# A state-space mixer with an MLP gate: one small product in two column halves, two broadcasts by DMA, and another order of the work

## The chip, the cores and the metric

One core of a Trainium2 chip runs the whole kernel. The time is the device time of one execution in microseconds. The kernel before was timed three times: 156.28 us in the median, from 156.19 to 156.82.

## What is computed

One sequence of 2048 rows with 448 features. The rows are normalized; a linear state-space scan and an MLP with GELU both read the normalized rows, and the MLP's SiLU gates the scan's output:

```python
xn  = layernorm(x)
dt  = exp(log_dt);  Lam_bar = exp(dt * Lambda)            # complex, 448 states
B_bar = ((Lam_bar - 1) / Lambda)[:, None] * B
Bu  = einsum("bld,pd->blp", xn, B_bar)
h_t = Lam_bar * h_{t-1} + Bu_t                            # over 2048 rows
s   = 2 * einsum("blp,dp->bld", h, C).real + xn * Dskip
y   = gelu(layernorm(xn) @ w1 + b1) @ w2 + b2             # 448 -> 1792 -> 448
out = x + s * silu(y)
```

All inputs and the output are bfloat16.

## The kernel before, in words

The rows go in four groups g of 512: two blocks b of 128 partitions, and in each partition two neighbouring rows, "par" 0 and 1. The scan runs over pairs of rows: an output row of par 1 needs the state after its pair (matrix CQ, seven 128-row pieces), a row of par 0 the state before it (CZ) and its own input through the direct matrix M0 (448 x 448, with D/2 on its diagonal).

The stages and their lines:
- Opening: loads, statistics (L402, L403), normalization (L423), transposes on TensorE (L426), short matmuls that only keep TensorE busy (L393), columns of b1 by matmul (L570, L571).
- First MLP product, `mm1_run` (L756). The contraction of 448 is split into row halves of the array, 64 rows each. Each pair of hidden blocks has a phase A of six matmuls and a phase B of eight, then two GELUs on ScalarE (L760) that free the two PSUM banks.
- Second MLP product, `mm2` (L778): fourteen matmuls of 448 columns. VectorE adds b2 (L781); for groups 0 and 3 ScalarE takes SiLU (L783), for 1 and 2 a tanh (L785) and a VectorE product (L786). ScalarE's function tables are switched between them (L414, L590, L594).
- `rows` (L576): two matmuls with one row each (L580) spread b2 and D over the partitions, into PSUM banks 6 and 5; copies (L581, L582) write b2bc and dbc (with the factor 0.5).
- Parameters of the scan (L496 on): small operations on 128x4 tiles on POOL or VectorE. A sine polynomial gives lr and li, from which come the combinations of B (`lb`, L635 and L637, then DMA transposes into BT) and of C (`cq`, L634 to L637: CQ0 to CQ6, CZ0 to CZ6).
- `m0` (L670): four pieces of the direct matrix, each seven matmuls of 448 columns (L673) and one short one for the diagonal (L675), copied by L390. The last piece, d = 3, has 64 rows.
- `bu` (L684): the scan's input, with BT0 to BT6, fourteen matmuls of 256 columns for each pair of pieces; copies u0 to u3 (L390).
- `ssm` (L696): products with the turning table WT, the scans (L708, L710) and products back into h, nearly all on VectorE; POOL or VectorE carry the end of a group over (L719 to L722).
- `ym` (L808): the output, L821 and L824 for par 0, L821 and L827 for par 1; then L833, L835 or L838 and the addition of x (L841) on VectorE or POOL, and the store.

The order of the work is written out by hand. The program makes a list of tasks, each with its reads and writes. `link` derives what each waits for. `ORDER` gives the order in which the tasks are issued, as numbers in that list, so every engine's queue is fixed; `SECOND` lists the tasks that take their second choice of engine. In `emit`, a task waits for one value of each semaphore that it needs and its engine has not waited for already. Every engine has one semaphore, every DMA one of its own. SP issues nearly all DMAs, among them the transposes; POOL issues the two loads of b1.

Of the kernel before, what the change touches and what calls it, by code (L numbers as in the profile page):

```python
# [7 lines left out]
ACT = mybir.ActivationFunctionType  # L8
# [27 lines left out]
class Plan:  # L36
# [69 lines left out]
    def emit(self):  # L106
# [5 lines left out]
        done = {}  # L112
        settle = [t for t in order if t.eng == "sp"][-5]
        for t in order:
# [25 lines left out]
            done[t] = (t.sem, self.counts[t.sem])  # L140
# [29 lines left out]
""".split()]  # L170
SECOND = [int(k) for k in """
29 52 54 58 61 63 70 71 72 75 76 79 80 83 84 86 87 88 89 106 130 133 135 161 163 164 188 192 193 196 228 230 232 244 248 252 253 263 273 336 348 353
361 371 373 375 385 398 399 400 433 441 443 446 447 465 479 480 484 488 492 496 498 501 505 507 522 527 528 586 602 628
# [4 lines left out]
X0 L1 N1 S1 W0 S0 R1 W1 Z0 B00 B01 M0 M1 B02 M2 B03 M3 X1 L2 B10 B11 B12 B13 R2 Y000 Y001 Y010 Y011 N2 W2 Z1 X2 L3 Y100 Y101 Y110 Y111 N3 Z2 X3 B20 B21 B22 B23 R3 S3 W3 B30 B31 B32 B33 Y200 Y201 Y210 Y211 Z3 Y300 Y301 Y310 Y311  # L178
# [12 lines left out]
def bass_recurrent_scan__ssm_conv_s5__mixer_channel_mlp__prompt_kernel(  # L191
# [17 lines left out]
    kb = Plan(nc)  # L209
    with ExitStack() as es:  # L210
# [84 lines left out]
        with nc.Block():  # L295
# [48 lines left out]
            for par in range(2):  # L344
                ld("sp", x_all[:, 0, par, :], dram_ap(A_x, par * D, [[2 * D, 128], [1, D]]), [f"x0p{par}"], 114688, S1)
# [12 lines left out]
            for k, vec in enumerate((B_b2, A_Dskip)):  # L358
                ld("sp", vrows[64 + 32 * k:65 + 32 * k, 64:512], dram_ap(vec, 0, [[D, 1], [1, D]]), [f"vr{3 + k}"], 1000, 0)
# [29 lines left out]
            def copy(pairs, rd, wr):  # L389
                kb.either(("act", [lambda e, o=o, i=i: e.activation(o, i, ACT.Copy) for o, i in pairs]), ("dve", [lambda e, o=o, i=i: e.tensor_copy(o, i) for o, i in pairs]), rd, wr)  # L390
# [576 lines left out]
```

## Time and profile before

The profiled execution took 156.18 us; its span is 154.4 us and 1.78 us lie around it. The granted clock is 1.0 throughout. From the page and the answers of the trace:

| what | value |
|---|---|
| timed runs | 156.28 us (156.19 to 156.82) |
| profiled execution / span | 156.18 / 154.4 us |
| ScalarE, POOL busy | 94.9 us (61%), 34.6 us (22%) |
| L756, 462 matmuls | 45.2 us |
| L778, 224 matmuls | 44.4 us |
| L684, 196 matmuls | 24.0 us |
| L821, 110 matmuls | 22.4 us |
| first L756 / end of the last matmul of the chain | 6.95 / 149.99 us |

"Busy" counts the time in which an instruction of an engine runs; matmuls are pipelined and their ends are modelled, so the distance from one to the next is often shorter than the stated length. The same holds on VectorE, where an operation of 0.68 us is often followed after 0.60. The chain of waits goes back from the last instruction to what released each step; a step that is on it sets the end.

### The profile page before, as it was taken

The page shows a single profiled execution, that of the slowest core. Times are in us where ns is not written, and L with a number is a line of the kernel's source. Part 1 is how long each engine was busy: PE and PEld are TensorE (multiplying, and loading weights), DVE is VectorE, ACT ScalarE, POOL GpSimd, SP SyncE. Part 2 cuts the span into 40 slices and gives each one's busy share as a digit, 9 for nine tenths or more (in the row PEclk, how much of TensorE's full clock was granted, in tenths as well). Part 3 has the DMA queues.
Part 4 walks back from the last instruction along what each step waited for, and adds up shares of the span by engine and source line. Part 5 has one row for each costly group of instructions (what it writes and reads, how often), then busy time and mean ns, then how long its engine had stood idle before and what let it go on. Part 6 is the DMA issues. An engine that isn't in the chain of part 4 may idle for free.

```text
span 154.4 us, 3113 instructions
## 1 busy us (share of the span) xinstructions
PE 149.3 (97%) x1140; PEld 89.0 (58%) x1140; DVE 134.9 (87%) x290; ACT 94.9 (61%) x178; POOL 34.6 (22%) x81
## 2 busy tenths in 40 slices
PE   7999999999999999999999999989999999999991
PEld 6777855455566576645444556755455565655561
DVE  3859899499898999999989998998989376999974
ACT  3797998988977757918927870115378661473200
POOL 6125850121300000000013950720030070002012
PEclk9999999999999999999999999999999999999999
DMA  4999669889893062200011310380031001000122
GB/s 121 290 310 373 182 140 261 148 156 219 183 172 69 4 125 84 46 4 2 0 39 25 59 59 7 62 185 4 0 59 59 6 0 62 0 0 4 59 111 69
DMA packets 31146, 14.52 MB, mean 94 GB/s; under 512 B 24722, under 2 KB 30746, under 8 KB 31130
## 3 DMA queue, kind: packets, MB, share of 16 engines
q1 hardware_dynamic: 30916, 14.26, 39.3%
q8 instruction: 9, 0.15, 0.4%
q10 hardware_dynamic: 150, 0.05, 0.1%
q14 instruction: 7, 0.06, 0.1%
q0 software_dynamic: 64, 0.00, 0.0%
HBM read 6.66 MB, written 1.84 MB: 55 GB/s over the span
## 4 chain that ended last, share of the span: by engine, by line
PE 92%; DVE 4%; issue 1%; ACT 1%; POOLq 0%; DVEq 0%
PE psum L756 28%; PE psum L778 28%; PE psum L684 12%; PE psum L821 12%; PE psum L824 4%; PE psum L673 4%; PE psum L393 3%; DVE g_sb L786 1%; PE psum L426 1%; PE psum L827 1%; DVE vs L722 1%; DVE xn_sb L467 1%; DVE t L835 1%; ACT gT L760 1%; DVE t L838 0%
## 5 line engine op out<-in xcount | busy, mean ns | idle before, releaser
L756 PE MATMUL psum<-xn2T,w_sb 64*128 64x512 bf16 (+1 forms) x462 | 45.2, 345 | 0.3
L778 PE MATMUL psum<-w_sb,gT 128*128 128x448 bf16 x224 | 44.4, 353 | 0.0
L760 ACT ACTIVATE gT<-psum,b1f 128x512 bf16<-128x512 f32 (+1 forms) x66 | 36.1, 625 | 10.1 <-PE psum L756 10.0
L756 PEld LDWEIGHTS psum<-xn2T,w_sb 64*128 64x128 bf16 x462 | 25.4, 109 | 18.7 <-issue 3.4
L778 PEld LDWEIGHTS psum<-w_sb,gT 128*128 128x128 bf16 x224 | 21.8, 98 | 20.1 <-issue 0.6
L684 PE MATMUL psum<-xnT,BT 128*128 128x256 bf16 x196 | 24.0, 273 | 0.1
L390 ACT ACTIVATE u_sb<-psum 128x512 bf16<-128x512 f32 (+2 forms) x20 | 9.9, 496 | 20.0 <-PE psum L684 20.0
L684 PEld LDWEIGHTS psum<-xnT,BT 128*128 128x128 bf16 x196 | 18.6, 98 | 5.7 <-issue 1.5
L841 POOL TENSOR_TENSOR tmp<-t,x_all 128x448 bf16<-128x448 bf16 x7 | 8.8, 1274 | 31.6 <-DVE t L838 25.5
L708 DVE TENSOR_TENSOR_SCAN s_w<-dk,vs 128x774 f32<-128x774 f32 x8 | 14.1, 1759 | 0.0
L821 PE MATMUL psum<-CZ,h_sb 128*128 128x448 bf16 x56 | 11.9, 353 | 0.5 <-DVE Cr L833 0.5
L390 ACT ACTIVATE vs<-s_w 64x256 bf16<-64x256 f32 (+2 forms) x14 | 7.8, 567 | 6.5 <-DVE s_w L710 5.6
L781 DVE TENSOR_TENSOR o<-psum,b2bc 128x448 f32<-128x448 f32 x16 | 9.8, 619 | 2.1 <-PE psum L778 2.0
L719 POOL TENSOR_TENSOR ang<-s_w,ang 128x16 f32<-128x16 f32 x3 | 1.0, 330 | 45.4 <-ACT s_w L717 45.4
L468 ACT ACTIVATE xn_sb<-x_all,lnw 128x448 bf16<-128x448 bf16 (+2 forms) x16 | 9.8, 651 | 2.0 <-DVE lnw L453 0.7
L821 PE MATMUL psum<-CQ,h_sb 128*128 128x448 bf16 (+2 forms) x54 | 10.5, 332 | 0.0
L786 DVE SCALAR_TENSOR_TENSOR g_sb<-th,o 128x448 bf16<-128x448 f32 x8 | 6.6, 823 | 4.3 <-ACT th L785 4.3
L467 DVE TENSOR_SCALAR xn_sb<-x_all,lnw 128x448 bf16<-128x448 bf16 (+2 forms) x24 | 8.7, 393 | 0.1
L783 ACT ACTIVATE g_sb<-o 128x448 bf16<-128x448 f32 x8 | 4.5, 571 | 6.8 <-DVE o L781 6.7
L821 PEld LDWEIGHTS psum<-CZ,h_sb 128*128 128x128 bf16 x56 | 5.3, 98 | 5.4 <-DVE Cr L833 0.8
L634 ACT ACTIVATE tmp<-Cr,cw 128x448 f32<-128x448 bf16 (+1 forms) x11 | 7.2, 665 | 1.7 <-DVE CQ L637 1.3
L821 PEld LDWEIGHTS psum<-CQ,h_sb 128*128 128x128 bf16 x54 | 5.1, 98 | 4.0 <-DVE vs L703 0.4
(159 smaller groups left out, 197.3 us busy)
## 6 DMA issues: line engine op xcount, KB each, us to landing
out_dram<-tmp SPq DMA_DIRECT2D x7, 224.0 KB, 1.9
x_all<-in_A_x_dram SPq DMA_DIRECT2D x3, 448.0 KB, 4.1
w_sb<-in_B_w_dram SPq DMA_DIRECT2D x3, 448.0 KB, 7.0
w_sb<-in_B_w_dram SPq DMA_DIRECT2D x3, 384.0 KB, 5.0
vs<-in_A_C_re_dram SPq DMA_DIRECT2D x1, 392.0 KB, 4.4
Bn<-in_A_B_re_dram SPq DMA_DIRECT2D x1, 336.0 KB, 7.9
Bn<-in_A_B_im_dram SPq DMA_DIRECT2D x1, 336.0 KB, 8.2
vs<-in_A_C_im_dram SPq DMA_DIRECT2D x1, 336.0 KB, 4.1
```

The costliest lines, as they stand in the source:

```text
L390: kb.either(("act", [lambda e, o=o, i=i: e.activation(o, i, ACT.Copy) for o, i in pairs]), ("dve", [lambda e, o=o, i=i: e.tensor_copy(o, i ...
L467: on = [("dve", [lambda e, o=o, i=i: e.tensor_scalar(o, i, rs, nb, op0=ALU.mult, op1=ALU.add) for o, i in parts], 0.4, 0.12), ("act", [lam ...
L468: ("act", [lambda e, o=o, i=i: e.activation(o, i, ACT.Identity, bias=nb, scale=rs) for o, i in parts], 0.75, 0.2)]
L684: fns = [lambda e, r=r, m=m, d=d: e.matmul(psum[:, 4, r * NK:(r + 1) * NK], BT[:, m, d, :], xnT[:, gx, d, :], start=(d == 0), stop=(d == 6 ...
L708: dve(lambda e, so=so, vi=vi: e.tensor_tensor_scan(so, dk[:].rearrange("p i c -> p (i c)"), vi, 0.0, ALU.mult, ALU.add), ["v", "vl", "dk", ...
L756: return lambda e: e.matmul(view(bk[k]), w1_sb[rows, d, fcol(2 * j + k)], rhs[rows, d, :, :], start=not second and n == 0, stop=second and ...
L760: act([lambda e, k=k: e.activation(gT[:, gb, 2 * j + k, :].rearrange("p (r c) -> p r c", r=2)[:, :, cols], view(bk[k]), ACT.Gelu_apprx_tan ...
L778: fns = [lambda e, fi=fi: e.matmul(psum[:, bk, 0:D], gT[:, gb, fi, q * 128:(q + 1) * 128], w2_sb[:, fi, :], start=(fi == 0), stop=(fi == N ...
L781: dve(lambda e: e.tensor_tensor(o2[:, fb, :], psum[:, bk, 0:D], b2bc[:], ALU.add), [f"ps{bk}", "b2bc"], [f"oo{fb}"], 0.62, prio - 76)
L786: dve(lambda e: e.scalar_tensor_tensor(out=g_sb[:, gs, :], in0=th[:, fb, :], scalar=1.0, in1=o2[:, fb, :], op0=ALU.add, op1=ALU.mult), [f" ...
L821: fns = [lambda e, k=k: e.matmul(psum[:, bk, c0:c1], h_sb[:, hb, k, k0:k0 + 128], cm[:, k, c0:c1], start=(k == 0), stop=False) for k in ra ...
L841: add = lambda e: e.tensor_tensor(o_sb[:, ob, par * D + c0:par * D + c1], t3[:, fb, c0:c1], res, ALU.add)
```

## The change

Five things:
- `m0` for d = 3 becomes `m0_halves`: the seven matmuls go alternately to output partitions 0 to 63 and 64 to 127 of one bank, the diagonal one to the second half. The second half is copied to a tile in SBUF, and VectorE adds the two into M0.
- b2 and D are spread over the partitions by two DMA loads from POOL's queue, and D is halved in place; `rows` is not called any more, and SP's two small loads go.
- `emit`: a task's needs are sorted by the place of their producers in the order (DMAs count as 24 places later). What the producer's engine had itself waited for counts as known, so some waits are left out; those that stay are issued with the latest last.
- The step list keeps its content: the switches of ScalarE's tables are named in another way and fall on the same groups (SiLU for 0 and 3). The switch for group 3 no longer waits for the tiles th.
- New `ORDER` and `SECOND`.

```diff
@@ emit
-            need = {}
-            for d in t.deps:
+            waits = []
+            for d in sorted(t.deps, key=at.get, reverse=True):
                 sem, val = done[d]
-                if need.get(sem, 0) < val:
-                    need[sem] = val
-            for sem, val in need.items():
                 if seen.get(sem, 0) < val:
-                    eng.wait_ge(self.sems[sem], val)
-                    seen[sem] = val
+                    waits.append((sem, val))
+                    for s, v in knows[d].items():
+                        learn(seen, s, v)
+                    learn(seen, sem, val)
+            for sem, val in reversed(waits):
+                eng.wait_ge(self.sems[sem], val)
+            base = dict(seen)
...
-            done[t] = (t.sem, self.counts[t.sem])
+            done[t], knows[t] = (t.sem, self.counts[t.sem]), base
@@ loads
-            for k, vec in enumerate((B_b2, A_Dskip)):
-                ld("sp", vrows[64 + 32 * k:65 + 32 * k, 64:512], dram_ap(vec, 0, [[D, 1], [1, D]]), [f"vr{3 + k}"], 1000, 0)
+            ld("pool", b2bc[:], dram_ap(B_b2, 0, [[0, 128], [1, D]]), ["b2bc"], 114688, -50, reads=["sgn3", "w1r_3"])
+            ld("pool", dbc[:], dram_ap(A_Dskip, 0, [[0, 128], [1, D]]), ["dbc"], 114688, -20, reads=["b2bc"])
+            kb.either(("act", lambda e: e.activation(dbc[:], dbc[:], ACT.Copy, scale=0.5), 0.6, 0.2),
+                      ("dve", lambda e: e.tensor_scalar(dbc[:], dbc[:], 0.5, None, op0=ALU.mult), 0.2, 0.12), ["dbc"], ["dbc"], -20)
@@ direct matrix
+            def m0_halves(bank):
+                BM = (3, 0, 4, 1, 5, 2, 6)
+                fns = [lambda e, k=k, m=m: e.matmul(psum[k % 2 * 64:k % 2 * 64 + 64, bank, 0:D], Bn[:, m, D + 384:896], CQ[:, k, :], start=(k < 2), stop=(k == 6))
+                       for k, m in enumerate(BM)]
+                fns.insert(6, lambda e: e.matmul(psum[64:128, bank, 384:D], ident[:, 0:64], De[:, 3, 0:64], start=False, stop=True))
+                pe(fns, [...], [f"ps{bank}"])
+                k = tslot[0] % 2
+                tslot[0] += 1
+                copy([(tmp[0:64, k, :], psum[64:128, bank, 0:D])], [f"ps{bank}"], [f"tmp{k}"])
+                dve(lambda e: e.tensor_tensor(M0[0:64, 3, :], psum[0:64, bank, 0:D], tmp[0:64, k, :], ALU.add), [f"ps{bank}", f"tmp{k}", "M0p"], ["M03"])
...
             def m0(d, bank, prio):
                 n = (128, 128, 128, 64)[d]
+                if d == 3 and 1:
+                    return m0_halves(bank)
@@ main program
             first_apply(1)
-            rows()
```

More of the change, by code (lines that the diff above doesn't have):

```diff
@@ L111, in emit, with learn @@
         assert len(order) == len(set(order)) == len(self.tasks)
-        done = {}
+        done, knows = {}, {}
+        at = {t: i + (24 if t.sem not in ENGS and not t.sem.startswith(("gelu", "silu")) else 0) for i, t in enumerate(order)}
         settle = [t for t in order if t.eng == "sp"][-5]
+        def learn(seen, sem, val):
+            if seen.get(sem, 0) < val:
+                seen[sem] = val
         for t in order:
@@ L344, in bass_recurrent_scan__ssm_conv_s5__mixer_channel_mlp__prompt_kernel @@
             for par in range(2):
-                ld("sp", x_all[:, 0, par, :], dram_ap(A_x, par * D, [[2 * D, 128], [1, D]]), [f"x0p{par}"], 114688, S1)
+                ld("sp" if par or not 0 else "act", x_all[:, 0, par, :], dram_ap(A_x, par * D, [[2 * D, 128], [1, D]]), [f"x0p{par}"], 114688, S1)
             ldx(1, 1, S1 + 2)
@@ L387, in tcols, with copy @@
                 return xn2_sb[:, b, a:a + 128]
-            def copy(pairs, rd, wr):
+            def copy(pairs, rd, wr, by=None):
+                if by is not None:
+                    kb.either(("act", [lambda e, o=o, i=i: e.activation(o, i, ACT.Copy, scale=by) for o, i in pairs]),
+                              ("dve", [lambda e, o=o, i=i: e.tensor_scalar(o, i, by, None, op0=ALU.mult) for o, i in pairs]), rd, wr)
+                    return
                 kb.either(("act", [lambda e, o=o, i=i: e.activation(o, i, ACT.Copy) for o, i in pairs]), ("dve", [lambda e, o=o, i=i: e.tensor_copy(o, i) for o, i in pairs]), rd, wr)
@@ L422, in first_apply @@
                     key = xk(0)[par:par + 1] if b == 0 else xk(1)
-                    dve(lambda e, src=src, dst=dst, mean=mean, r1=r1: e.tensor_scalar(dst, src, mean, r1, op0=ALU.subtract, op1=ALU.mult),
+                    parts = [(dst, src)] if b == 0 or not 0 else [(dst[:, 0:384], src[:, 0:384]), (xn2_sb[:, b, par * 512 + 384:par * 512 + 512], src[:, 320:D])]
+                    dve([lambda e, o=o, i=i, mean=mean, r1=r1: e.tensor_scalar(o, i, mean, r1, op0=ALU.subtract, op1=ALU.mult) for o, i in parts],
                         key + [f"r1{q}", f"mv0_{q}"], [f"xm{b}p{par}"])
+                    if b and 0:
+                        if par:
+                            kb.dma("sp", xn2T[:, 0, :, 128:256], xn2_sb[:, 1, :], reads=["xm1p0", "xm1p1", "xm1"], writes=["xmT1p0", "xmT1p1"], transpose=True)
+                        continue
                     bank, oap = 6 - par, xn2T[:, 0, par * 4:par * 4 + 4, b * 128:b * 128 + 128]
@@ L590, in silu_table, with gelu_again @@
                 kb.add("act", lambda e: e.preload_act_table_set("silu_and_others"), rd, [f"Ws{g}"], sem=f"silu{g}")
-            def gelu_again():
-                kb._sem("gelu")
-                kb.add("act", lambda e: e.preload_act_table_set("gelu_apprx_tanh_and_others"), ["W"] + [f"g{n}" for n in range(4)], ["Wg"], sem="gelu")
+            def gelu_again(g):
+                kb._sem(f"gelu{g + 1}")
+                kb.add("act", lambda e: e.preload_act_table_set("gelu_apprx_tanh_and_others"), ["W"] * (g == 0) + [f"g{n % 8}" for n in range(4 * g, 4 * g + 4)] * (9 >> g & 1), [f"Wg{g + 1}"], sem=f"gelu{g + 1}")
             def tables():
@@ L844, in part @@
                     on = [("dve", add, 0.1 + (0.28, 0.47)[par] * w / D, 0.12), ("pool", add, 0.2 + 1.1 * w / D, 0.15)]
-                    kb.either(*on, rd, [f"o{ob}_{par}_{c0}"], prio)
+                    if last and par or 1:
+                        kb.either(*on, rd, [f"o{ob}_{par}_{c0}"], prio)
+                    else:
+                        dve(add, rd, [f"o{ob}_{par}_{c0}"], on[0][2], prio)
                     if last:
@@ L871, in bass_recurrent_scan__ssm_conv_s5__mixer_channel_mlp__prompt_kernel @@
             first_apply(1)
-            rows()
-            mm1_run(0, None, range(N1, 7), [j % NP for j in range(N1, 7)])
+            if N1 < 7:
+                mm1_run(0, None, range(N1, 7), [j % NP for j in range(N1, 7)])
             mm1_run(0, 1, range(N1), [(j + 7) % NP for j in range(N1)])
@@ L922, in bass_recurrent_scan__ssm_conv_s5__mixer_channel_mlp__prompt_kernel @@
                 elif k == "S":
-                    if g == 0:
-                        gelu_again()
-                    if g == 3:
-                        silu_table(3, [f"gT1_{fi}_{b}" for fi in range(NF) for b in range(2)] + ["th0", "th1"])
+                    if a == "g" and wg(g + 1) == g + 1:
+                        gelu_again(g)
+                    if a == "s" and silu_now(g):
+                        silu_table(g, [f"gT{g % 2}_{fi}_{b}" for fi in range(NF) for b in range(2)])
                 elif k == "M":
```

17 lines of the change are left out of this document (10 added, 7 removed), and 34 rows, old and new, of the table ORDER.

## The prediction

> **What bounds the kernel.** I read four views. The page's first lines come first, because they tell which engine has no room left.
>
> ```profile
> span 154.4 us, 3113 instructions
> PE 149.3 (97%) x1140; PEld 89.0 (58%) x1140; DVE 134.9 (87%) x290; ACT 94.9 (61%) x178; POOL 34.6 (22%) x81
> PEclk9999999999999999999999999999999999999999
> ```
>
> TensorE is busy 97% at the full granted clock, so nothing can come from the clock. VectorE, at 87%, is the one that can stop it. Then I read the chain of work that ended last, in order of time (start, us, what).
>
> ```profile
> 17.34 0.29 PE psum L580 x2
> ...
> 61.44 1.44 PE psum L673 x7
> 62.88 0.03 PE psum L675
> ...
> 100.43 0.55 DVE Cr L833
> 100.98 0.05 issue
> 101.03 1.50 PE psum L821 x7
> ...
> 119.04 1.64 PE psum L684 x14
> ...
> 126.87 1.53 PE psum L684 x14
> ...
> 149.99 0.03 issue
> ```
>
> From 1.12 to 149.99 us the chain is nearly all TensorE, back to back; 4.4 us of VectorE, POOL and the last store follow. So an edit is worth what it takes from TensorE's stream, or puts into it as a wait. Third, the waits, to see how much of the stream is idle:
>
> ```profile
> PE psum L821 <- DVE Cr L833: 0.5, 1, 0.5
> ```
>
> This is the largest wait of a matmul after the start. The chain around it goes through VectorE from 96.2 to 101.0, and the fourth view, VectorE's timeline, shows why VectorE is late there:
>
> ```profile
> 96.91 2.02 POOL L841 TENSOR_TENSOR tmp<-t,x_all 128x448 bf16<-128x448 bf16 x2 [6.02 <-DVE vs L722]
> 96.95 1.03 DVE L722 TENSOR_TENSOR vs<-cur,vs 128x6 bf16<-128x6 f32 x1
> ```
>
> The same operation takes 0.18 at 80.89. While POOL works on 128x448 tiles here, three VectorE operations in a row (L722, L467, L786) each take about 0.8 longer than elsewhere.
>
> The sums go against the profiled execution: 156.18, that is the span of 154.4 and 1.78 around it. It lies 0.10 under the median of 156.28, and I add this 0.10 at the end.
>
> **The change, part by part.** I numbered the tasks by the program's text, before and after, and read both orders engine by engine.
>
> *Broadcasts.* The two L580 matmuls go: the chain gives 0.29, with the changes of form on both sides. ScalarE has its L581 copy (0.58) out of that stretch and another normalization (0.65) in, behind the two GELU pairs that free the banks TensorE still needs, so I take -0.29 (bounds -0.29 and 0). In place come two loads on POOL's queue and a scaling on ScalarE (0.58, as L581). The first load waits for a w1 load, the second for the first; both must be issued before POOL goes on to the sine polynomial. The trace has no load of 112 KB from POOL; the nearest rows are POOL's b1 loads (0.53 to 0.79 to issue, 2.9 and 3.8 to landing) and SP's 112 KB loads (2.1). The w1 load is issued at about 5.7 and lands, as the 64 KB rows do, 4.6 to 5.1 later; then come 0.8, 3 to 4 and 0.5 for the two loads, so the sine starts at 14.5 to 16 instead of 12.7. Late next would be the Bn combinations and through them the transposes; VectorE reaches its first need (lr) only near 20.5 in the new order, and the polynomial takes 3.1. That is the cover; if the load landed only after 7.0, like the 448 KB rows, 1 to 2 us would come onto VectorE there, of which the transposes (done 3 us ahead of the first L756 that reads them) and the table switch hide all but some 0.3. I take 0 (bounds 0 and +0.3).
>
> *The last 64 rows.* Now seven 448-column matmuls and a short one take 1.47 (61.44 to 62.91). In two column halves four go to one half and three and the short one to the other. No row shows column halves. From below: the row halves of L756 run in pairs, so that the chain has 84 of 512 columns in 9.38, 0.112 each, where L778 at full width has 14 of 448 columns in 2.65, 0.189 each, which would be 0.216 for 512. With that overlap it is 4 x 0.189 = 0.76, and 0.87 with the 0.11 of a change of form (next part). From above: no overlap, 1.47. I take 0.87, so -0.60 (bounds -0.71 and 0). The new copy and add (0.5 and 0.6 on VectorE) are counted below. The result is needed only at the first L824, ten us later.
>
> *Changes of form.* After row-split work (L756) fourteen L684 take 1.64 against 1.53 elsewhere, and L756 after full-width work starts some 0.05 slow: 0.16 for a pair. The new order has nine row-split stretches of L756 down to seven (the L580 pair and the column halves are counted above): -0.32, taken as -0.30 (bounds -0.32 and 0). The Trainium skill, "TensorEngine Tiling (Array Packing)", Key Properties, says that a change of tiling mode drains the array; the trace agrees, at 0.11 and 0.05, and by that rule the column halves, now put between row-split matmuls, pay on both sides too.
>
> *Opening.* On POOL an iota (0.37) and a select now stand ahead of the second b1 load, and another select between the loads. That load starts 0.34 later; before, it was issued at 2.43 and landed 3.8 later, at 6.23, and L570 that reads it ran at 6.36. So +0.20 (bounds 0 and +0.35). The w1 copy that the second L756 group waits for also moves back, by 0.2, and fits behind this delay.
>
> *Order: the waits that go.* 0.48 at 101.0 and 0.15 at 39.8: -0.50 (bounds -0.63 and 0).
>
> *Order: the waits that come.* Walked with distances from start to start in VectorE's timeline (L637 0.60, L781 0.54, stats 0.56, 1536-wide products 0.95, scans 1.68):
> - From the end of the product with BT2 and BT5 to the first L673 TensorE has 2.65 + 0.77 + 2.65 = 6.07. VectorE, which must now cast u2 itself, has 0.2 + 0.54 + 0.54 + 0.2 + 0.95 + 0.56 + 0.60 + 0.95 + 0.60 + 0.1 + 0.60 = 5.84 until CQ6. Room: 0.2.
> - From the same point to the first L821 TensorE has 30.2. VectorE has 30.3 until CZ6: scan stage 11.3, ten L637 6.0, stats 2.2, casts 1.7, bias adds 1.6, normalizations 1.6, next scan's products 1.8, L786 1.1, L634's work taken over 1.1, small ones 1.3, the new add 0.6. Room: about -0.1. Before, CZ6 was done at 75.6 for a start at 77.0.
> - At the last scan, TensorE has 2 x 2.65 + 0.77 + 2.09 + 2.65 + 1.33 + 2.65 = 14.8 from the third L684 group to the L821 that needs h; VectorE needs 13.6. Before it was 16.1 for 15.9, without a wait. Better.
>
> I take +0.40 for all of them (bounds 0 and +3.2, below).
>
> *Waits in the order of events, and fewer.* In the chain "issue" is 0.7% of the span, 1.1 us, and 0.79 of it is the start. I take -0.05 (bounds -0.3 and 0).
>
> Sum: -0.29 + 0 - 0.60 - 0.30 + 0.20 - 0.50 + 0.40 - 0.05 = -1.14, so 155.04, and 155.1 for the median.
>
> **Rivals.**
> - *The new waits eat the gain.* Both tight places on VectorE cost some 0.6 each instead of 0.4 together, and the 0.5 at 101 comes again, as the same bank (7) passes through the same L833. 155.1 + 0.8 + 0.5 = 156.4. For it: room of 0.2 and -0.1; against: TensorE idled only about 1 us in the order before, with room as small at the last scan.
> - *Column halves run one after the other*, so that part does not do what it says: 155.1 + 0.6 = 155.7. For it: no row shows it; against: the pairs of row halves. The Trainium skill, "TensorE: Matmul & The Clock Gate", Part 3, gives 2.38 times for three column tiles; this trace cannot show it.
> - *VectorE becomes the bound between 48 and 79 us, and the kernel gets slower.* POOL gets whole-tile products (xd of blocks 1 and 2) and a normalization's power chain there, which VectorE did before. If four VectorE operations are stretched by 0.8 each, as at 97 to 100, CZ6 is 3.2 late and the first L821 waits that long: 155.1 + 3.2 - 0.4 = 157.9. It decides from an excess of about 2.3 on. For it: the rows at 97; against: POOL's power row beside VectorE at 85.5 to 87.5 stretched nothing, and the xd products may fall before 48, where VectorE waits for TensorE anyway. The Trainium skill, "SBUF — State Buffer", Who interferes with whom, says that a VectorE instruction with two SBUF inputs contends with a GpSimd one that reads SBUF. The L722 and L786 rows agree; L467, with one input, was stretched as well.
>
> **How the numbers follow.** The measurement tells a change from none at about 0.5%, 0.78 us: 155.5 and 157.06 are the borders. Forecast (154.0 to 155.5 is its own range: all bounds of gain at once, -0.29 - 0.71 - 0.32 - 0.63 - 0.3, give 156.28 - 2.25 = 154.0): 0.64, all faster. Waits eat it: 0.17, and serial halves: 0.05, both within. VectorE the bound: 0.14, slower. The range from 154.0 to 156.9 holds all but the last.
>
> **What would show it.** L580 absent and the chain without 0.29 there; the 64-row products as eight matmuls within 0.9 us; the first L570 at 6.5 to 6.6; no 0.5 wait at the L821 near 100; waits of a few tenths at the first L673 and the first L821, ended by L637. It is wrong if TensorE's waits on VectorE sum to over 1.2, if the halves take 1.4, or if POOL's loads hold up lr.

## The result: 157.88 us, slower by 1.1%

| | before | changed |
|---|---|---|
| median of the timed runs | 156.24 us (156.19 to 156.82) | 157.88 us (157.77 to 158.57) |
| ratio, 95% interval | 1 | 1.0106 (1.0069 to 1.0143) |
| profiled execution / span | 156.18 / 154.4 us | 157.85 / 155.9 us |

The forecast was 155.1 us with a range to 156.9. Ratios, here and below, are formed over undisturbed runs, the medians over all, so the two can differ by some tenths of a per cent.

The line numbers have moved: L756 is now L789, L760 L793, L778 L814, L684 L717, L673 L706 (L692 for the column halves), L821 L857, L785 L821, L637 L656, L634 L653, L390 L404 and L467/L468 L486/L487. The page of the changed kernel begins:

```profile
span 155.9 us, 3004 instructions
PE 148.4 (95%) x1138; PEld 87.1 (56%) x1138; DVE 134.4 (86%) x289; ACT 92.4 (59%) x170; POOL 44.9 (29%) x92
```

TensorE's busy time fell from 149.3 to 148.4 us, so the work that was to go did go. The granted clock stays at 1.0. The waits of the matmuls (who waits for whom: total, times, longest) tell the rest:

```profile
PE psum L706 <- ACT M L404: 1.3, 1, 1.3
...
PE psum L789 <- ACT gT L793: 0.5, 2, 0.3
PE psum L445 <- DVE xn_sb L438: 0.4, 1, 0.4
PE psum L717 <- ACT u_sb L404: 0.4, 1, 0.4
PE psum L789 <- DMA w_sb<-in_B_w_dram: 0.3, 1, 0.3
```

That is 2.9 us, where the kernel before had one wait of 0.5 behind its start. 0.9 less work and 2.4 more waiting make the 1.5 by which the span grew. L404 is the copy out of a PSUM bank, L793 the GELU that writes gT. Three of the five waits are for ScalarE, and the one for VectorE is not among those that the forecast had watched. The chain that ended last shows why (start, us, what):

```profile
5.66 5.19 DMA w_sb<-in_B_w_dram
...
11.43 6.26 DMA b2bc<-in_B_b_dram
...
17.98 0.61 POOL dbc L84
...
32.82 4.92 DMA xnT<-xn_sb
...
55.98 2.38 POOL lnw L466
...
58.39 2.07 ACT xn_sb L487 x4
...
60.94 1.50 PE psum L706 x7
```

Before, 92% of this chain was TensorE; now it is 59%. Up to 60.94 us the chain does not touch TensorE at all: a w1 load, the b2 broadcast, POOL's sine polynomial behind the second broadcast, the sines and table switches, a transpose load, the combinations on VectorE, POOL's normalization scale, ScalarE, and only then a matmul. From 60.94 on it is TensorE again. Two DMAs on it were put down at nothing or not at all: the b2 broadcast, 6.26 us, and the transpose load of xn_sb, 4.92. VectorE's timeline shows who stands behind the second one:

```profile
37.84 0.83 DVE L486 TENSOR_SCALAR xn_sb<-x_all,lnw 128x448 bf16<-128x448 bf16 x2 [4.03 <-DMA xnT<-xn_sb]
```

L486 writes the next normalized block into xn_sb, which the transpose has to read first. In the kernel before that transpose was issued at 25.85 us; the new order puts it behind two BT and two Ct transposes on SP, at 32.82, and SP's transposes go one after the other at 1.3 us each.

### The profile page after: what moved, and what is told of

It is laid out like the page before. It is cut to its first block, busy times and chain, and to the rows that moved or that the text cites. A ratio compares the mean times of both kernels' runs of the same rounds, so it can differ in the third digit from the quotient of the medians.

```text
span 155.9 us, 3004 instructions
## 1 busy us (share of the span) xinstructions
PE 148.4 (95%) x1138; PEld 87.1 (56%) x1138; DVE 134.4 (86%) x289; ACT 92.4 (59%) x170; POOL 44.9 (29%) x92
## 4 chain that ended last, share of the span: by engine, by line
PE 59%; DVE 11%; DMA 11%; ACT 6%; POOL 6%; issue 3%; SPq 3%; DVEq 0%; POOLq 0%
PE psum L814 15%; PE psum L789 14%; PE psum L857 13%; PE psum L717 9%; DMA b2bc<-in_B_b_dram 4%; PE psum L860 4%; DMA w_sb<-in_B_w_dram 3%; DMA xnT<-xn_sb 3%; SPq L84 3%; ACT WT L635 2%; DVE CQ L656 2%; PE psum L706 2%; DVE tmp L654 2%; POOL lnw L466 2%; DVE lnst L388 1%
## 5 line engine op out<-in xcount | busy, mean ns | idle before, releaser
L789 PE MATMUL psum<-xn2T,w_sb 64*128 64x512 bf16 (+1 forms) x462 | 45.4, 346 | 1.0 <-ACT gT L793 0.5
L814 PE MATMUL psum<-w_sb,gT 128*128 128x448 bf16 x224 | 44.4, 353 | 0.0
L793 ACT ACTIVATE gT<-psum,b1f 128x512 bf16<-128x512 f32 (+1 forms) x66 | 36.0, 623 | 7.2 <-PE psum L789 7.0
L789 PEld LDWEIGHTS psum<-xn2T,w_sb 64*128 64x128 bf16 x462 | 24.4, 109 | 20.8 <-ACT gT L793 3.2
L814 PEld LDWEIGHTS psum<-w_sb,gT 128*128 128x128 bf16 x224 | 21.7, 98 | 19.8 <-issue 0.6
L717 PE MATMUL psum<-xnT,BT 128*128 128x256 bf16 x196 | 24.0, 273 | 0.4 <-ACT u_sb L404 0.4
L404 ACT ACTIVATE u_sb<-psum 128x512 bf16<-128x512 f32 (+2 forms) x20 | 9.3, 463 | 22.4 <-PE psum L717 22.2
L717 PEld LDWEIGHTS psum<-xnT,BT 128*128 128x128 bf16 x196 | 18.7, 98 | 5.9 <-issue 2.0
L877 POOL TENSOR_TENSOR tmp<-t,x_all 128x448 bf16<-128x448 bf16 x5 | 6.7, 1349 | 40.8 <-DVE t L874 26.6
L741 DVE TENSOR_TENSOR_SCAN s_w<-dk,vs 128x774 f32<-128x774 f32 x8 | 14.6, 1852 | 0.0
L404 ACT ACTIVATE vs<-s_w 64x256 bf16<-64x256 f32 (+2 forms) x13 | 9.7, 744 | 7.4 <-DVE s_w L741 5.0
L486 DVE TENSOR_SCALAR xn_sb<-x_all,lnw 128x448 bf16<-128x448 bf16 (+2 forms) x29 | 9.6, 366 | 4.3 <-DMA xnT<-xn_sb 4.0
L857 PE MATMUL psum<-CZ,h_sb 128*128 128x448 bf16 x56 | 11.9, 353 | 0.0
L653 ACT ACTIVATE tmp<-Cr,cw 128x448 f32<-128x448 bf16 (+1 forms) x11 | 7.3, 664 | 5.6 <-DVE CQ L656 3.1
L857 PE MATMUL psum<-CQ,h_sb 128*128 128x448 bf16 (+2 forms) x54 | 10.5, 332 | 0.0
L857 PEld LDWEIGHTS psum<-CZ,h_sb 128*128 128x128 bf16 x56 | 5.3, 98 | 4.9 <-DVE CZ L656 0.4
L487 ACT ACTIVATE xn_sb<-x_all,lnw 128x384 bf16<-128x384 bf16 (+2 forms) x11 | 6.5, 635 | 2.3 <-POOL lnw L466 2.3
L860 PE MATMUL psum<-M,xnT 128*128 128x448 bf16 x32 | 7.4, 353 | 0.0
L857 PEld LDWEIGHTS psum<-CQ,h_sb 128*128 128x128 bf16 x54 | 5.2, 98 | 3.7
L388 DVE BATCH_NORM_STATS2 lnst<-x_all 128x6 f32<-128x448 bf16 x12 | 7.2, 618 | 0.0
L833 POOL TENSOR_TENSOR xd<-xn_sb,dbc 128x448 bf16<-128x448 bf16 x5 | 5.2, 1038 | 5.1 <-DVE tmp L654 5.1
```

Source lines behind the costliest of these rows:

```text
L388: dve([lambda e, b=b, par=par, q=q: e.bn_stats(lnst[:, q, :], x_all[:, 2 * g + b, par, :])], [f"x{2 * g + b}"] , [f"st{q}"], 0.62, prio)
L486: on = [("dve", [lambda e, o=o, i=i: e.tensor_scalar(o, i, rs, nb, op0=ALU.mult, op1=ALU.add) for o, i in parts], 0.4, 0.12), ("act", [lam ...
L653: on = [("act", [lambda e, o=o, i=i, c=c: e.activation(tmp[o, k, :], b[i], ACT.Copy, scale=c[i]) for o, i, c in ps], 0.66 * len(ps), 0.2), ...
L717: fns = [lambda e, r=r, m=m, d=d: e.matmul(psum[:, 4, r * NK:(r + 1) * NK], BT[:, m, d, :], xnT[:, gx, d, :], start=(d == 0), stop=(d == 6 ...
L741: dve(lambda e, so=so, vi=vi: e.tensor_tensor_scan(so, dk[:].rearrange("p i c -> p (i c)"), vi, 0.0, ALU.mult, ALU.add), ["v", "vl", "dk", ...
L789: return lambda e: e.matmul(view(bk[k]), w1_sb[rows, d, fcol(2 * j + k)], rhs[rows, d, :, :], start=not second and n == 0, stop=second and ...
```

## The experiments

Theories: T1, the transpose load that is late on SP; T2, POOL's two broadcast loads, whose waits hold up the sine polynomial; T3, the rival on record, VectorE stretched beside POOL; later Q, ScalarE's queue, and V, VectorE as the next bound. All times are medians of 6 to 12 runs, each beside the kernel before on its own chip (156.2 to 156.4). A profile shows one of these runs only, and not always one near the median: those of a2, d2 and g2 are the slowest of their twelve.

| run | from | edit | us | ratio to before, 95% |
|---|---|---|---|---|
| a1 | changed | transpose load earlier | 157.19 | 1.0047 (1.0022 to 1.0072) |
| a2 | changed | POOL's loads without waits | 156.83 | 1.0035 (1.0010 to 1.0061) |
| a3 | changed | a1, a2 and the old order of the first w1 loads | 155.67 | 0.9950 (0.9922 to 0.9977) |
| a4 | before | column halves alone | 156.60 | 1.0022 (1.0006 to 1.0037) |
| b1 | a3 | M copy first on ScalarE | 156.06 | 0.9964 (0.9937 to 0.9992) |
| b2 | a3 | full width again | 156.77 | 0.9980 (0.9947 to 1.0014) |
| b3 | changed | M copy first on ScalarE | 157.78 | 1.0076 (1.0053 to 1.0099) |
| c1 | before | broadcasts alone | 162.73 | 1.0381 (1.0336 to 1.0425) |
| c2 | before | broadcasts alone, no waits | 156.28 | 0.9988 (0.9959 to 1.0018) |
| d1 | a3 | M copy, one L487 pair, u copy first | 155.18 | 0.9910 (0.9877 to 0.9943) |
| d2 | a3 | scale of group 2 on VectorE | 156.15 | 0.9964 (0.9930 to 0.9998) |
| d3 | d1 | full width again | 156.21 | 0.9983 (0.9957 to 1.0010) |
| f1 | d1 | second M copy earlier | 155.73 | 0.9969 (0.9948 to 0.9990) |
| f2 | d1 | transpose load late again | 155.79 | 0.9970 (0.9950 to 0.9991) |
| f3 | d1 | POOL's loads wait again | 156.32 | 0.9992 (0.9972 to 1.0012) |
| f4 | changed | d1's order of ScalarE alone | 157.68 | 1.0090 (1.0062 to 1.0119) |
| g1 | d1 | first w1 loads in the changed order | 155.64 | 0.9961 (0.9938 to 0.9983) |
| g2 | d1 | POOL's negation early | 155.44 | 0.9951 (0.9931 to 0.9971) |

### The two DMAs, each alone and together (a1, a2, a3)

a1 moves one task (168 is the transpose load), a2 takes two reads away, a3 does both and puts task 22 before 23, the first w1 column load before the row load:

```diff
@@ a1: ORDER
-... 164 167 75 64 194 ... 279 249 168 196 ...
+... 164 167 168 75 64 194 ... 279 249 196 ...
@@ a2
-["b2bc"], 114688, -50, reads=["sgn3", "w1r_3"])
-["dbc"], 114688, -20, reads=["b2bc"])
+["b2bc"], 114688, -50)
+["dbc"], 114688, -20)
@@ a3: ORDER, with both
-... 94 23 25 104 97 2 49 98 50 108 22 100 ...
+... 94 22 23 25 104 97 2 49 98 50 108 100 ...
```

> One move in SyncE's order: the transpose load of normalized x for the odd half of group 0 (it reads xn_sb) goes right behind its twin, ahead of the BT and Ct loads instead of behind them. Theory T1: in the changed kernel this transpose landed at 37.74 us (25.85 was its issue before), and the next normalization into xn_sb (L486) waited 4.03 us for it on VectorE; the statistics, POOL's power chain and ScalarE's queue inherit that, and TensorE waits 1.3 us at L706 and 0.4 at L717. By T1 the 4.03 wait and both TensorE waits go: 157.9 - 1.7 = 156.2 us. Theory T2 (POOL's two broadcast loads delay the sine polynomial by 6 us, and that is what makes VectorE and ScalarE late): 157.9, with the wait moved but the 1.3 still there. Theory T3 (VectorE stretched by POOL's products between 48 and 79 us, as the rival in the prediction had it): 157.9, same waits.

> The two broadcast loads on POOL's queue no longer wait (the b2 load waited for the fourth w1 row load, 2.31 us, the D load 3.92 for the b2 load). They are issued back to back and the sine polynomial follows. T2: the sine starts at about 13.0 instead of 18.63, the GELUs of group 1 begin 1 us earlier and the matmul waits at 35 to 37 us (0.5 in all) go; if the lateness of VectorE and ScalarE at 48 to 61 us also comes from there, the time falls by 2 to 156. T1: only the 0.5 goes, 157.4, and the 4.03 wait on the transpose load stays. T3: 157.4 too, with the 1.3 at L706 kept.

> Both moves of the two kernels before it, and on SyncE the first w1 column load again ahead of the first w1 row load (in the changed kernel it stood behind, and the first L789 began at 7.47 us, against 6.95 before). If the parts add up (1.7 from the transpose load, 0.5 from the loads on POOL, 0.4 from the opening): 157.9 - 2.6 = 155.3 us, faster than the kernel before by 0.6%. By T2 alone 155.6, by T3 157.0 (the opening and the 0.5 only).

a1 gave 0.7 and not 1.7. Its waits of matmuls:

```profile
PE psum L706 <- ACT M L404: 1.0, 1, 1.0
PE psum L789 <- ACT gT L793: 0.5, 2, 0.3
PE psum L814 <- DVE cw L548: 0.3, 1, 0.3
```

The wait at L717 is gone, L706 lost only 0.3, and 0.5 at gT is still there. VectorE's 4.03 is gone too, but the next in the same queue is late instead:

```profile
40.08 0.63 DVE L654 TENSOR_SCALAR tmp<-Cr,cw 128x448 f32<-128x448 bf16 x1 [2.97 <-DMA Cr<-vs]
```

The transposes of C now stand where the one of xn_sb stood. So T1 names a real wait and priced it at more than twice its worth. a2 gave 1.05: the sine polynomial started at 14.03 instead of 18.63 and the waits for gT went, as T2 says, though its profile kept 1.3 at L706. Together and with the w1 order it is 2.2; the two alone are 1.75, and g1 below gives the w1 order 0.5, so the medians do not show that each of the two hides the other. The traces point to it: POOL's L466, which ScalarE waits for, starts at 55.98 in the changed kernel, at 55.36 in a1, 56.04 in a2 (where the first L789 is 1 us later) and 53.67 in a3.

T3 is not the whole cause, since a3 has all of VectorE's work and is faster than before. But the stretch that it names was there, beside POOL's product for xd (L833) from 43.71 us on:

```profile
43.70 1.52 DVE L656 SCALAR_TENSOR_TENSOR CQ<-Cr,cw,tmp 128x448 bf16<-128x448 bf16 x1
```

Elsewhere this operation takes 0.68. With two L654 before it (1.11 and 0.65 instead of 0.45) that is 1.7 us. The same three long operations stand in the profiles of a2, b3, f2 and f4, the kernels that have the late transpose too. With the early one both products fall some 3 to 6 us earlier, mostly where VectorE waits; there d2 and g2 have two long operations, the others at most one L654. So a part of what the late transpose costs may be this stretch; how much of it reached the end was not tried.

### The broadcasts in the kernel before (c1, c2)

The same edit as in the change, put into the kernel before; the loads stand ahead of the sine polynomial on POOL. c2 leaves out the two `reads=`, as a2 does.

```diff
@@ main program of before
-            rows()
@@ ORDER, numbers shifted: 9 sgn3, 44 and 45 the loads, 61 the sine polynomial
+... 12 9 44 45 61 ...
```

> The kernel before with the broadcasts of b2 and D alone: the two row loads and the two L580 matmuls with their copies go, and the two 112 KB loads come onto POOL's queue ahead of the sine polynomial with the waits that the change gives them; the scaling goes to ScalarE where the second copy stood. The prediction's term: -0.29, so 156.0. Theory T2: the polynomial starts 5 to 6 us later, the sines and the table switch with it, and the GELUs of group 1 hold TensorE up by what freeing the loads gave in the changed kernel (157.88 to 156.83): 156.25 - 0.3 + 1.0 = 157.0.

> The kernel before with the broadcasts of b2 and D alone, as in the run that gave 162.73 us, but the two loads wait for nothing: issued at about 9.8 and 10.4, the sine polynomial right behind them (near 11 instead of 18.1), the b2 load landed near 16.5 (6.7 us in the kernel with freed loads), the first bias add in this order at 23.3. Theory W (the waits in POOL's queue are the cost, the loads themselves are not): 156.3 - 0.3 = 156.0. Rival L (the loads on a queue that is fed by POOL cost by themselves, through the other loads or through a late b2): 157 or more.

c1 cost 6.4 us, far over what T2 gave. Its largest wait of a matmul, the two issues on POOL, and two stretches (busy time of each engine, then PEclk, DMA share and GB/s):

```profile
PE psum L780 <- DVE o L783: 4.3, 1, 4.3
```

```profile
11.07 0.65 POOL L84 DMA_DIRECT2D b2bc<-in_B_b_dram  x1 [1.44 <-DMA w_sb<-in_B_w_dram]
17.57 0.54 POOL L84 DMA_DIRECT2D dbc<-in_A_Dskip_dram  x1 [5.84 <-DMA b2bc<-in_B_b_dram]
```

```profile
20.00:31.00 11.00, 6.70 (x32) 3.17 (x31) 7.53 (x26) 8.11 (x14) 6.56 (x20) 0.87 0.58 120
31.00:41.00 10.00, 10.00 (x57) 4.53 (x56) 6.09 (x16) 6.48 (x10) 1.42 (x8) 0.80 0.85 150
```

VectorE waits 4.45 for the polynomial until 21.32 and 2.04 for POOL's next chain, the bias add L783 (at 28.63) stands behind both in its queue, and TensorE waits 4.3 for the bias add. In these two stretches the granted clock is 0.87 and 0.80 in the mean; in pieces of 2 us it is 0.50 from 29 to 35 us and 1.00 behind them. The first twenty L780 behind the wait take 6.67 us, 2.9 more than at the usual 0.19 each. The two are 7.2; with the 0.3 of L580 against them that is 6.9, and this profiled execution is 6.8 longer than that of the kernel before. The Trainium skill, "TensorE: Matmul & The Clock Gate", Part 1, says that the clock is set by how busy the array has been; this is the one trace here that shows it. Without the waits (c2) the loss is gone: 156.28, ratio 0.9988. So the waits were the cost. The gain of 0.29 does not show in the time: first L758 to first L780 takes 12.51 us instead of 12.70, but this execution's opening was 0.36 longer.

### The column halves (a4, b2, d3)

a4 is the kernel before with `m0_halves` (the copy goes to a tile hm of its own); b2 and d3 are a3 and d1 with the following, the rest of the order as it was (without the add, so the numbers behind it shift by one):

```diff
-                if d == 3 and 1:
+                if d == 3 and 0:
```

> The kernel before, with the last 64 rows of the 448-row products in two column halves and nothing else changed (the second half's copy goes to a tile of its own, ScalarE takes it, VectorE adds; both stand in the order right behind the matmuls). In the changed kernel the whole of it took about 0.81 us on TensorE against 1.47. If that saving is real and its copy and add are covered: 156.24 - 0.6 = 155.6. If the copy and the add (about 0.5 and 0.6 us) come onto the path through VectorE or ScalarE: 156.2 or more.

> The kernel with both moves and the w1 order (155.67 us), with the last 64 rows at full width again, as one group of eight matmuls and one copy (no second half, no add on VectorE). If TensorE is what bounds the stretch from 60 to 80 us, the column halves are worth the 0.65 that the chain shows and the time rises to 156.3. If VectorE bounds it, as in the kernel before with the halves alone (156.6, no gain), the time stays at 155.7 or falls by up to the 0.6 of the add.

> The kernel with the new ScalarE order, with the last 64 rows at full width again. It tells what the column halves are worth where nothing else waits near 58 us: 154.7 + 0.65 = 155.4 if TensorE bounds the stretch from 60 to 80 us; 154.7 or less if VectorE does (the halves cost it an add of 0.6).

The chains of d1 and d3 give the size of the saving on TensorE, first with the halves:

```profile
69.03 0.72 PE psum L692 x7
69.74 0.09 issue
```

and at full width:

```profile
69.20 1.44 PE psum L706 x7
70.64 0.03 PE psum L708
```

0.81 against 1.47: the halves do overlap. As a time it depends on the order around them. In d1 they are worth 1.0 (155.18 and 156.21 on one chip), of which the chain accounts for 0.66; in these two profiles 0.4 more is an "issue" of 0.40 before VectorE's last addition, which d3's chain has, like that of the kernel before, and d1's has not. Beside a3 it cannot be told from none: b2's twelve runs lie between 155.05 and 157.45, and its interval overlaps with a3's. In the kernel before they gain nothing (a4), and its chain says why:

```profile
54.70 0.04 DVE o L794
...
83.75 0.53 DVE Cr L846
...
84.33 1.50 PE psum L834 x7
```

From 54.70 to 84.28 us it is VectorE's. TensorE had the 0.6 (from the first product with CQ to the next group's first MLP matmul 16.63 us instead of 17.22). It gave some of it back on the way to the first L834 (10.71 instead of 10.48) and at two waits of 0.4 for L846 (before, one of 0.5); the rest is an opening longer by 0.5 in this execution. The new add is one more VectorE operation, and by this chain VectorE had no room for it in the old order; that the add itself is what costs was not tried.

### ScalarE's queue (b1, b3, d1, f1, f4)

In the changed kernel ScalarE stands so:

```profile
58.39 2.07 ACT L487 ACTIVATE xn_sb<-x_all,lnw 128x384 bf16<-128x384 bf16 x4 [2.29 <-POOL lnw L466]
60.37 0.52 ACT L404 ACTIVATE M<-psum 128x448 bf16<-128x448 f32 x1
```

The M copy needs nothing of L487, but stands behind it, and the bank that it empties is the one that the next L706 writes. The edits move tasks 327 (M copy), 377 (u copy) and 329 (second M copy) against 373 and 370 (L487):

```diff
@@ ORDER: b1 on a3, b3 on the changed kernel
-... 335 336 373 370 232 88 234 326 268 338 376 327 374 309 339 ... 377 ...
+... 335 336 232 88 234 326 268 338 376 327 373 370 374 309 339 ... 377 ...
@@ d1 on a3, f4 on the changed kernel
+... 376 327 373 377 370 374 309 339 ...
@@ f1 on d1
-... 345 379 312 159 ... 242 329 472 ...
+... 345 329 379 312 159 ... 242 472 ...
```

> The kernel with both moves and the w1 order (155.67 us) and one more move, on ScalarE alone: the copy of the first 128 rows of the 448-row product (M, L404) goes ahead of the two L487 normalizations that stood before it. In the trace of that kernel TensorE still waits 1.01 us at L706 for this copy; the copy stands behind four L487, which wait for POOL's chain L462 to L466 (50.16 to 56.04 us), whose last small instruction took 2.37 us there and 0.47 at 72.8. Theory Q (a queue matter: the copy needs nothing of the normalization): the 1.0 goes, 155.67 - 1.0 = 154.7. Rival V (VectorE is as late as TensorE there, and the time comes back as a wait for CZ or u a few us later): 155.3 to 155.7.

> The changed kernel (157.88 us) with the move on ScalarE alone: the M copy ahead of the two L487 normalizations. Its TensorE waits 1.3 us for this copy. Theory Q: 157.88 - 1.3 = 156.6. Rival V (VectorE, 4 us late from the transpose load, sets the pace a few us later anyway): 157.3 to 157.9, and the wait turns up at another line.

> The kernel with both moves and the w1 order (155.67 us), and on ScalarE the order M copy, one L487 pair, the copy of the next u, then the other L487 pairs (the move of the M copy alone only handed TensorE's wait of 1.0 us on to that u copy, as 1.2 at L717). Nothing but ScalarE's order changes. Theory Q (only ScalarE's queue holds TensorE up near 58 us): no wait at L706 or L717, 155.67 - 1.0 = 154.7. Rival V (VectorE reaches its own needs later than TensorE from 60 us on): the wait comes back at L857 or L814 and the time stays at 155.4 to 155.8.

> The 155.18 us kernel (both moves, w1 order, ScalarE's order) with one more copy moved on ScalarE: that of the second 128 rows (M, 64.61 us in its trace) ahead of a tanh (0.56) and an L653 (0.66). TensorE still waited 0.49 us for it at L706 (64.70 to 65.19). Theory Q: the 0.49 goes, 154.7. Rival V (VectorE bounds from here on): the wait turns up at L717 or L857, 155.0 to 155.3.

> The changed kernel (157.88 us) with ScalarE's whole new order alone (M copy, one L487 pair, u copy, the other pairs). Theory Q (the 1.3 at L706 is ScalarE's queue): 157.9 - 1.1 = 156.8. Theory T1 (VectorE and POOL are 2 us later there, so L487 itself starts only at 58.4 and the u copy behind one pair at 59.5): 157.3 to 157.6.

b1 and b3 missed: the wait went on to the next copy in the same queue, L717 for u (1.2 and 1.5 in all). d1 puts that copy ahead too and has the lowest median of the case, 155.18, though its interval overlaps with a3's. Its matmuls wait for one thing behind the start:

```profile
PE psum L706 <- ACT M L404: 0.5, 1, 0.5
```

This is not the copy that a3 waited for but the next one, of the second 128 rows, at 65.19 us. Moving it as well (f1, 155.73) only made another late: f1's profile has 1.0 at L717, for a u copy behind an L653 that waits 0.75 for VectorE. So it is partly V. On the changed kernel itself ScalarE's order gave nothing that can be told from none (b3 and f4, 157.78 and 157.68). POOL's L466 starts at 56.17 and 57.24 in their profiles, in d1's at 53.67; that this lateness is the reason is likely, and not shown.

### Why ScalarE waits: POOL's scale chain (d2, g2)

The same VectorE instructions run in a3 and, 0.16 us earlier, in b2, beside POOL's L466, an operation on 128x8 numbers. In a3 POOL and then VectorE have:

```profile
53.67 2.37 POOL L466 TENSOR_SCALAR lnw<-lnw 128x8 f32<-128x8 f32 x1
```

```profile
53.52 0.67 DVE L656 SCALAR_TENSOR_TENSOR CQ<-Cr,cw,tmp 128x448 bf16<-128x448 bf16 x1
54.11 0.94 DVE L734 TENSOR_TENSOR vs<-pa,pb 128x1536 bf16<-128x1536 bf16 x1
...
55.52 0.41 DVE L735 TENSOR_TENSOR pa<-u_sb,WT 128x512 bf16<-128x512 bf16 x1
...
55.93 1.76 DVE L741 TENSOR_TENSOR_SCAN s_w<-dk,vs 128x774 f32<-128x774 f32 x1
```

In b2:

```profile
53.51 0.62 POOL L466 TENSOR_SCALAR lnw<-lnw 128x8 f32<-128x8 f32 x1
```

In a3 POOL's instruction ends at 56.04, 0.1 behind the start of the scan, after a row of products with two inputs each; in b2 it got through 0.1 behind the end of the first of them, and there the wait at L706 is gone. Of the fourteen profiles that have this instruction at that place, thirteen have 2.37 or 2.38, and in all of these it ends 0.1 behind the start of the scan. In all fourteen, b2 too, it starts 0.15 behind the same L656 (0.16 in one), so the row of VectorE's operations alone does not decide it.

```diff
@@ d2: SECOND
+369
@@ g2: POOL's chain
-                               lambda e: e.tensor_tensor(w(3), mean2, w(2), ALU.mult),
-                               lambda e: e.tensor_scalar(w(3), w(3), -1.0, None, op0=ALU.mult)]
+                power = fns + [lambda e: e.tensor_scalar(lnw[:, b, 1, 0, qs], mean, -1.0, None, op0=ALU.mult),
...
+                               lambda e: e.tensor_tensor(w(3), lnw[:, b, 1, 0, qs][:, None, :].to_broadcast([128, 2, nq]), w(2), ALU.mult)]
```

> The kernel with both moves and the w1 order (155.67 us), with the normalization scale of group 2 (POOL's L462 to L466, 5.9 us, of which its last instruction 2.37) as ten small operations on VectorE instead (about 0.17 each, 1.9 in all). Theory P (POOL is locked out by VectorE's two-input products between 53.7 and 56.0 and that is what makes ScalarE late): ScalarE's L487 start near 52 to 53 instead of 56.1 and the wait of 1.0 at L706 goes, 154.7; VectorE is 1.9 later from there on, and where that shows the time is 155.5 to 156.5. Rival (the 2.37 is POOL's own): the same start of L487 without any change at other places.

> The 155.18 us kernel with POOL's scale chain in another order: the negation (L466, 2.37 us at the end of the chain) is applied to the mean ahead of the power, so that the product is the last instruction; the same count of instructions, the same values. Theory P (POOL is locked out while VectorE's two-input products run back to back from 53.5 to 55.9): the negation at 51.3 takes 0.2 to 0.8, and whatever stands last now is held until the scan begins only if it starts behind 53.5; the chain ends between 53.9 and 56.0, L487 starts with it, and the time is 154.7 to 155.2. Rival (the instruction is slow by itself): the negation takes 2.4 at its new place and the chain ends at 56 as before, 155.2.

In g2 the negation (now L464, on half as many numbers) takes a tenth of the time:

```profile
52.95 0.22 POOL L464 TENSOR_SCALAR lnw<-lnmv 128x4 f32<-128x4 f32 x1
53.25 1.94 POOL L465 TENSOR_TENSOR lnw<-lnw,mhalf 128x8 f32<-128x8 f32 x1
55.27 0.57 POOL L466 TENSOR_TENSOR lnw<-lnw 128x8 f32<-128x8 f32 x1
```

The chain takes 4.1 us instead of 5.9. With b2's 0.62 for the same instruction, this says that the 2.37 was not the instruction's own. But theory P, that the row of products keeps POOL out until the scan, is not borne out as it stands: g2's last instruction, L466 at 55.27, starts 0.16 behind the L656 that leads the same row there, and takes 0.57, though the scan starts only at 57.52. The Trainium skill, "SBUF — State Buffer", Who interferes with whom and Summary, says that a VectorE instruction with two SBUF inputs and a GpSimd instruction that reads SBUF shut each other out, whoever is first, until the first has finished. The traces of b2 and g2 agree: POOL's instruction ends 0.1 behind the VectorE product that had started first. In the other thirteen it stayed out over four to five instructions in a row. What decides between the two stays open. d2 missed: the scale on VectorE pushed CQ back, and TensorE waited 1.4 for L656 instead. Neither moved the time below d1's. The profiles of both also lost time to a w2 load that came late, 0.9 in d2 and 1.7 in g2.

### What each is worth when the others are mended (f2, f3, g1)

> The 155.18 us kernel with the transpose load of the odd half of group 0 behind the BT and Ct loads again, as in the changed kernel. Theory T1: VectorE waits about 4 us near 34 for the transpose to read xn_sb, everything VectorE feeds at 48 to 61 us is 2 us later, and TensorE waits 1 to 1.5 us: 156.2 to 156.7. Rival (with ScalarE's order mended the lateness is absorbed): 155.2 to 155.5.

> The 155.18 us kernel with POOL's two broadcast loads waiting again (the first for the fourth w1 row load, the second for the first). Theory T2: the sine polynomial starts near 18.6 instead of 14, the GELUs of group 1 hold TensorE up 0.5 near 35 to 37, and VectorE is later by 1 at 48: 155.7 to 156.5. Rival (hidden now): 155.2.

> The 155.18 us kernel with the first w1 row load ahead of the first w1 column load on SyncE, as in the changed kernel. Theory O (the column load, 192 KB, is what the first L789 waits for, and lands later when the row load goes first): the first L789 0.3 to 0.8 later and the time 155.5 to 156.0. Rival (the opening is set by the x load and varies from run to run whatever the order): 155.2.

From 155.18, the waits of POOL's loads cost 1.1 (f3; 0.5 at gT is back), the late transpose 0.6 (f2), the w1 order 0.5 (g1). In f2's profile the mechanism of T1 does not reach TensorE any more:

```profile
35.26 0.83 DVE L486 TENSOR_SCALAR xn_sb<-x_all,lnw 128x448 bf16<-128x448 bf16 x2 [1.49 <-DMA xnT<-xn_sb]
```

1.49 instead of 4.03, with TensorE fully busy from 31 to 60 us; its loss of 0.7 is a wait for a w2 load. g1's profile starts its first L789 at 7.26, d1's at 7.54, so theory O is not shown: the first L789 starts between 7.10 and 7.54 in the ten profiles with the old order of the w1 loads, and between 7.26 and 8.43 in the six with the changed one, of which only two are above 7.54 (a2, f4). f2 and g1 ran on other chips than d1 and differ from it by little more than their spread; only f3 is clear.

## Why the prediction was wrong, step by step

- **Changes in TensorE's work: right.** L580 is gone, the halves took 0.81 (forecast 0.87), and busy time fell by 0.9 against 1.19 for the three terms. The changes of form (-0.30) and the order of the waits (-0.05) were not tried singly. What was wrong was to take the halves' copy and add as covered: alone (a4) they gain nothing, and by a4's chain VectorE had no room.
- **Broadcasts, taken at 0 (bounds 0 and +0.3): the largest error.** The mechanism was named, its size was off. The first load was issued at 11.43 and took 6.26 us, near the 448 KB rows and not POOL's 3 to 4. The 3 to 4 holds where little else is loaded: in c1 the second load took 3.3 while the DMA engines moved 71 GB/s, the first 6.2 at 351. The polynomial started at 18.63, not at 14.5 to 16, and VectorE waited 0.9 for lr: the sign of being wrong that the prediction had named. The cover was priced from VectorE's first need of lr alone; the sines, the second table switch and the GELUs of group 1 stand behind it too. Measured: 1.05 (a2) and 1.1 (f3).
- **Opening, +0.20: not settled.** The b1 matmuls ran at 6.46, a little ahead of the forecast. In this execution the first L789 started 0.52 later than before; it waited 0.3 for w1 itself, whose column load now stands behind the row load, and a transpose 0.4 for the normalization of x. The forecast had only the w1 copy for the second group in view. But the first matmul of this kind starts at 6.95 in the profile of the kernel before and at 7.49 in a4, whose opening is the same, so one profile does not tell the change from the spread, and g1 does not either.
- **Waits that go, -0.50: right.** TensorE is busy without a gap from 83 to 108 us.
- **Waits that come, +0.40: wrong in place and cause.** Where VectorE's operations were counted against TensorE's, little came: the first L706 began 0.2 late, its weight load waiting for CQ, and at the first L857 the weight load waited 0.4 for CZ without making the matmul late. The 1.7 came at an L717 (48.75) and at the second L706 (60.94), through three queues: SP's transposes, POOL's chain, ScalarE's copies. The walk was made engine by engine for the data that a matmul reads. It left out that L486 must wait for the last reader of xn_sb, and that a copy which frees a bank stands behind whatever its queue holds.
- **The rival at 157.9 came out in the number, not in the mechanism.** VectorE was stretched, by 1.7 us from 41 to 45 and not by 3.2 from 48 on, and CZ was in time for the first L857. At 56 to 58.4 it was POOL that was late. That the total is 157.9 is luck.

With four places of the order and two waits put right, d1 has all parts of the change and runs in 155.18, near the 155.1 forecast; it gets there by other terms than the forecast's, with a wait of 0.5 at L706 and an unsettled opening. How the 2.7 between 157.88 and 155.18 is shared is known in part. The 1.1 for POOL's loads is measured from both ends. The medians give 0.6 to 0.7 to the late transpose, 0.5 to ScalarE's order (a3 to d1) and 0.5 to the w1 order, and the four add up to 2.7. But the last three are hardly larger than the spread, and ScalarE's order alone is worth 0.1 to 0.2 on the changed kernel (b3, f4), so these three shares are not shown.

## What to carry to other kernels

When an order is changed, walk for every moved instruction its last readers too, not only its sources: a transpose load moved back holds the next writer of its input, and a copy that frees a bank is only as early as the slowest thing ahead of it in its queue. A load with an artificial wait blocks its whole issuing queue: price what stands behind it. And a saving on one engine counts only where that engine is on the chain; look whether the other engine has room for what the saving costs it.

## What the hardware showed that was not expected

- POOL's 128x8 operation took 2.37 us beside a row of two-input VectorE products in thirteen profiles, 0.62 beside the same row in b2, and in the same profiles 0.47 or 0.48 at its next place, between 71 and 76 us. It ended 0.1 us behind the start of the scan in all thirteen. What let it in earlier in b2 is open.
- VectorE's operations were long beside POOL's 128x448 products: 1.52 instead of 0.68 with two inputs, 1.11 instead of 0.45 for an L654 with one.
- The two 112 KB loads that POOL issued while the w1, w2 and B loads ran took 6.0 to 7.0 us each, with the waits (changed kernel) or without (a2), and up to 8.2 in g2; SP's first x loads, of that size, took 2.1 (2.3 in the changed kernel). In c1, where the DMA engines moved 71 GB/s meanwhile instead of the changed kernel's 173, POOL's second load took 3.3.
- With those loads free, a w2 load landed 10.5 us (d2, f2) and 11.5 us (g2) after its issue and held TensorE 0.7 to 1.7 us in three of the profiles (d2, f2, g2) and not at all in others of the same order. It may be the cause of the spread of over 1 us in these kernels' runs; that was not tried.
- After 4.3 us of idle time TensorE ran at a granted clock of 0.50 for about 6 us (c1, 29 to 35 us): one wait on the chain cost two thirds as much again.
